# Second products of the last but one group by Strassen's form, added onto rows that stay on the chip

## The chip, the cores and the metric

One Trainium2 chip; the kernel uses one of its cores. The metric is the device time of one execution in microseconds (us). The time before is the median of 3 runs: 692.39 us (691.91 to 694.4). The engines of the core are named as the profile names them: PE (TensorE, matrix products into the accumulator banks, PSUM), DVE (VectorE), ACT (ScalarE), POOL (GpSimd, which also issues the transfers that add) and SP (SyncE, which issues the other transfers). Each of them runs its own instructions in order and waits on semaphores for the others.

## The reference

One block over x of 2048 rows and 512 columns: a modulated layer norm, a two-sided discrete Fourier transform (real part), a gated residual, a second modulated layer norm, and a gated feed-forward network with a second gated residual.

```python
mod = (_silu(c) @ w_mod).reshape(c.shape[0], 6, 1, -1)
sa, ca, ga, sb, cb, gb = (mod[:, i] for i in range(6))
h = _layernorm(x) * (1 + ca) + sa
a, b = h @ dft_hid_re.T, h @ dft_hid_im.T
x = x + ga * (dft_seq_re @ a - dft_seq_im @ b)
h = _layernorm(x) * (1 + cb) + sb
x = x + gb * ((_silu(h @ w1) * (h @ w3)) @ w2)
```

w1 and w3 are 512 x 1792, w2 is 1792 x 512, all float32. The change lies in the last product, with w2.

## The kernel before

**Tiling.** Everything is kept with the hidden columns on the partitions. The 2048 rows are four blocks t = 0 to 3 of 512 rows; the 512 output columns are four blocks d of 128; the 1792 inner columns are seven groups g = 0 to 6 of 256 (NG = 7), each as two halves q of 128. Blocks are worked in pairs, `PAIRS = ((0, 2), (1, 3))` (L814): pair 1 is the blocks 1 and 3, and it comes last. The groups 0 and 1 of pair 0 are done singly; all the rest is a list of twelve items (L1175), (2..6, pair 0) and then (0..6, pair 1).

**A product** (L96 to L106) is three matmuls, since every float32 operand is split into a high and a low part of a faster type: high x high, high x low, low x high. ScalarE copies out the high parts, VectorE subtracts to get the low ones.

**First products.** For an item, `factor` (L1362) computes the products with w1 ("a") and w3 ("b") for both blocks and both halves with seven products instead of eight, in Strassen's way; "a5" or "b3" is one of these seven, six matmuls long. Some factors add onto a PSUM bank whose earlier content ScalarE or VectorE has to have read. `result` (L1240) hands SiLU(a) times b on to the second product: the plain form makes a high and a low part of each of four tiles; `seven_parts` (L1263) makes seven pairs of parts, of the four tiles, of differences of them, through VectorE.

**Second products.** `down_unit` (L1125) is the plain form: one unit is one (t, d), six matmuls, eight units per item. `seven_unit` (L1331) is Strassen's form: seven units of six matmuls per item, each on the banks 6 and 7; a unit that opens an accumulation starts them afresh (n = 2, 5, 1), the others (3, 6, 7, 4) add onto what the unit before left there. After each unit ScalarE copies both banks, times gb, to a tile y (`copy_by`, line L335 of the profile), and GpSimd issues a transfer that adds y to the rows in DRAM, `sums[t, which]`. The units come in the order n = 2, 5, 3, 1, 6, 7, 4 and go to the places (which, k) of `TO7`: the places (0, 0), (0, 1) and (1, 1) are hit twice, (1, 0) once, by the last. Strassen's form needs sums of w2's blocks beside w2, so its weights are prepared by five background jobs (`seven_jobs`, L1294), the plain form's by two (`plain_jobs`, L1217).

**The last two groups of pair 1.** `SEVEN` (L1226) holds the groups 0 to 4 of pair 1. After the last Strassen unit of group 4 `load_sums` (L1113) reads the rows back from DRAM into four resident tiles `xr` (transfers on SP). The groups 5 and 6 use the plain form, and VectorE adds each unit, times gb, to `xr` (`own`, L1147); for group 6 SP then stores the row tile to the output. The banks of these units rotate through 6, 7, 0, 1, 2 by a count of units, `turn[1]`, that runs on from the start of the feed-forward part.

**What sets the order.** The order of units is written out by hand as strings (L1799 to L1817): "a6 y a5" is a factor, a second-product unit taken from the queue `seconds`, a factor; "-b3" is the factor b3 of the item before. Within one engine instructions run in the order in which the program emits them. `behind(n, fn)` (L1073) delays a function by n units, so that, for example, the high part of a finished tile is copied at the head of the next unit, ahead of that unit's own copies out of the banks. The background jobs go out by `advance` (L117): each unit earns credit for VectorE and ScalarE (1.36 less a fixed use per kind of unit, L1683 to L1693), and jobs are issued from the head of the queue while the credit they need is above zero. `judge` (L1013) computes the flag that decides whether a slower general branch runs; it is emitted when nine units are left in `seconds`.

Buffers in SBUF are 50 slots (`take`, `give`), used again in turn; a slot that a transfer still reads holds up who writes it next.

Of the kernel before, what the change touches and what calls it, by code (L numbers as in the profile page):

```python
# [12 lines left out]
OP = mybir.AluOpType  # L13
# [8 lines left out]
NT = S // N  # L22
ND = D // P
NG = F // (2 * P)
# [18 lines left out]
def folded(nc, pools, c, cp, wmr, wmc, x, xt, ctr, cti, wdr, wdi, w1, w3, w2, out):  # L43
# [752 lines left out]
    xr = {}  # L796
# [17 lines left out]
    PAIRS = ((0, 2), (1, 3))  # L814
    h2h, h2l = {}, {}
    xc, sums = {}, {}
# [308 lines left out]
    def down_unit(g, pair, t, d, key):  # L1125
        last = g == NG - 1

        own = pair == 1 and g >= NG - 2
        if not own and d % 2 == 0:
            ys[0] = take(F32, "y")  # L1130

        parts = 2 if own and last and (t, d) == (NT - 1, ND - 1) else 1
        for n in range(parts):
            at = slice(n * N // parts, (n + 1) * N // parts)
            to = bank(down_banks[turn[1] % len(down_banks)])[:, at]
            turn[1] += 1
            for q in range(2):
                product(
                    to,
                    [u[:, q, cols(d)] for u in wuse[key]],  # L1140
                    [hf[g, t, q][:, b, at] for b in range(2)],
                    q == 0,
                    q == 1,
                )
            if own:
                xs = xr[t][d // 2][:, d % 2, at]
                nc.vector.scalar_tensor_tensor(  # L1147
                    xs, to, gb[:, d : d + 1], xs, op0=OP.mult, op1=OP.add
                )
                if last:  # L1150
                    nc.sync.dma_start(out[t, d, :, at], xs)
            else:
                if pair == 0 and 1 <= g * ND + d <= 4:
                    nc.vector.tensor_scalar(
                        ys[0][:, d % 2, :], to, gb[:, d : d + 1], None, op0=OP.mult
                    )
                else:
                    copy_by(ys[0][:, d % 2, :], to, gb[:, d : d + 1])
        if not own and d % 2 == 1:
            y = ys.pop(0)  # L1160
            nc.gpsimd.dma_start(sums[t, d // 2], y, accum_op=OP.add)  # L1161
            behind(4, lambda: give(y))
            if last:
                behind(8, lambda i=d // 2: store(t, i))
        if d == ND - 1:
            for q in range(2):
                give(hf.pop((g, t, q)))
            if t == PAIRS[pair][1]:
                give_w(key)
            if pair == 1 and g == NG - 3:  # L1170
                load_sums(t)
# [51 lines left out]
    TO = {1: 0, 6: 0, 7: 0, 4: 0, 2: 1, 5: 2, 3: 2}  # L1223
    state, vs = {}, {}

    SEVEN = [(g, 1) for g in range(NG - 2)]  # L1226
    ORDER7 = (2, 5, 3, 1, 6, 7, 4)
    LEFT7 = {1: "h0", 2: "h2", 4: "h3", 5: "s0", 6: "s1", 7: "s2", 3: "s3"}
    TO7 = {2: (0, 0), 5: (1, 1), 3: (0, 1), 1: (0, 0), 6: (0, 1), 7: (1, 1), 4: (1, 0)}
# [101 lines left out]
    def seven_unit(g, pair, n, key):  # L1331
        new = n in (1, 2, 5)
        if new:
            banks7[:] = [bank(6), bank(7)]
        y = take(F32, "y")
        which, k = TO7[n]
        t = PAIRS[pair][k]
        names = ("h", "l") if LEFT7[n][0] == "h" else ("sh", "sl")
        u = right7.pop(((g, pair), n))
        for e, to in enumerate(banks7):  # L1340
            at = int(LEFT7[n][1]) * HALF + e * P
            product(
                to,
                [flat(wuse[key][x])[:, at : at + P] for x in names],
                [u[:, b, :] for b in range(2)],
                new,
                True,
                not new,
            )
            d = 2 * which + e  # L1350
            copy_by(y[:, e, :], to, gb[:, d : d + 1])
        give(u)
        nc.gpsimd.dma_start(sums[t, which], y, accum_op=OP.add)  # L1353
        behind(4, lambda: give(y))
        if n == ORDER7[-1]:
            for x in wuse.pop(key).values():
                give(x)
            if g == NG - 3:
                for t in PAIRS[pair]:
                    load_sums(t)  # L1360
# [322 lines left out]
    USED = {"w1": (0.0, 0.5), "w3": (1.2, 0.5), "y": (0.0, 0.6), "own": (0.7, 0.0)}  # L1683
# [7 lines left out]
    def beside(us, used):  # L1691
        advance(us - used[0], us - used[1], jobs)
        if not jobs:  # L1693
            advance(0.0, 0.0)
# [9 lines left out]
    def down(g, pair, *which):  # L1704
        key = which[-1]
        drain(lambda: (key, "l") in done, jobs)
        delayed()
        if (g, pair) in SEVEN:
            seven_unit(g, pair, *which)
        else:  # L1710
            down_unit(g, pair, *which)
        beside(1.36, USED["own" if pair == 1 and g >= NG - 2 else "y"])

    for w in ("w1", "w3"):
        load_w((w, 1))
# [36 lines left out]
    def unit(kind, i, n):  # L1752
        g, pair = items[i]
        more = i + 1 < len(items)
        if n == 1:
            drain(lambda: ("ready", i, "w1" if kind == "a" else "w3") in done, jobs)
        if (kind, i, n) == ("a", 0, 6):
            drain(lambda: ("t", 0, 4) in done)
        if (kind, i, n) == ("a", turning, 1):
            drain(lambda: not background)  # L1760
        if kind == "a" and i == turning and n in (4, 5, 6, 7):
            drain(lambda: ("t", 1, {6: 2, 5: 1, 7: 3, 4: 4}[n]) in done, jobs)
        delayed()
        factor(i, "w1" if kind == "a" else "w3", n)
        if (kind, n) == ("a", 1):
            load_w(("w1", *items[i + 1]) if more else ("w2", g, pair))
        if (kind, n) == ("a", 6):
            load_w(("w2", g, pair))
        if not more and kind == "a" and state[i, "w1"]["n"] == 7:
            down_banks[:] = [6, 7, 0, 1, 2]  # L1770
        if (kind, n) == ("a", 7 if i == turning else 3) and more:
            load_w(("w3", *items[i + 1]))
            weight_jobs(i + 1, "w1")
        if (kind, n) == ("b", 2):
            (seven_jobs if (g, pair) in SEVEN else plain_jobs)(("w2", g, pair))
        if (kind, n) == ("b", 3):
            if i + 2 == turning:
                drain(lambda: ("xc", 3) in done)
                for at in ((1, 0), (1, 1), (3, 1)):
                    chunk_parts(background, *at, 3)  # L1780
                sums_of.append(pair_sums(background, 1))
            if i + 1 == turning:
                other_operands()
            if more and not early_w3(i):
                weight_jobs(i + 1, "w3")
            if (g, pair) in SEVEN:
                seconds.extend((g, pair, n, ("w2", g, pair)) for n in ORDER7)
            else:
                for t in PAIRS[pair]:
                    seconds.extend((g, pair, t, d, ("w2", g, pair)) for d in range(ND))  # L1790
        if (kind, n) == ("b", 6) and more and early_w3(i):
            weight_jobs(i + 1, "w3")
        beside(1.36, FACTOR[kind][n])
# [4 lines left out]
    for i in range(len(items)):  # L1798
        body = "a6 a5 y y a7 y a3 y a4 y b1 y b2 y b6 b5 y"  # L1799
        if i and items[i - 1] in SEVEN:  # L1800
            body = "a6 a5 a7 y a3 a4 y b1 b2 y b6 b5 y"
        if i == turning + 1:
            body = "a6 a5 y a7 a3 y a4 b1 y b2 b6 y b5"
        spread = i > 1 and items[i - 2] in SEVEN
        if spread and i < len(items) - 1:
            body = body.replace("a6", "a6 y", 1)
        if i == len(items) - 2:
            body = "a6 y a5 y a7 a3 y a4 b1 y b2 b6 y b5"
        if i == turning:
            body = "y y y y y a6 y a5 y a7 y b1 b2 a4 b6 a3 b5"  # L1810
        if i == len(items) - 1:
            body = "a6 a5 b1 a7 a3 b2 a4 y b6 y b5 y b7 y b4 y y b3 y y y y y y y y y y"
        head = "-b7 a1 -b4 -b3 a2 " if i == turning else "-b7 a1 a2 -b4 -b3 " if i else "a1 a2 "
        if spread and i < len(items) - 1:
            head = "-b7 a1 y a2 -b4 y -b3 "
        if i == len(items) - 1:
            head = "-b7 y a1 a2 y -b4 y -b3 "  # L1817
        for at in (head + body).split():
            if at == "y":
                if (i, len(seconds)) == (len(items) - 1, 9):  # L1820
                    judge()
                if (i, len(seconds)) == (len(items) - 1, 4):
                    tc.mark_branch_hint_location("general", hint="LikelyTaken")
                down(*seconds.popleft())
            elif at[0] == "-":
                unit(at[1], i - 1, int(at[2]))
            else:
                unit(at[0], i, int(at[1]))
# [804 lines left out]
```

## Time and profile before

| what | value |
|---|---|
| median of 3 runs | 692.39 us (691.91 to 694.4) |
| the profiled execution | 690.63 us |
| its span, first to last instruction | 688.8 us |
| PE busy | 672.4 us, 98% |
| DVE busy | 586.8 us, 85% |
| ACT busy | 451.2 us, 65% |
| POOL busy | 132.2 us, 19% |
| adds of y to the rows in DRAM | 63 of 512 KB, 5.7 us from issue to landing in the median |
| read-back of the rows | 4 of 512 KB, 4.3 us from issue to landing in the median |

The shares are of the span. Matmuls are pipelined, so the length of one PE row is more than the time that it takes of PE; what a unit takes is read from start to start. In a row of the order in time a bracket at the end is the engine's idle time before the instruction and what ended it. Lines such as L87, L90, L93, L96, L100 and L335 are helpers (a copy, a difference, a sum, an elementwise product, a matmul, a scaled copy); which work it is shows in the names of the tiles.

### The profile page before, as it was taken

What the parts mean: (1) busy time and instruction counts of PE and PEld (TensorE: products, weight loads), DVE (VectorE), ACT (ScalarE), POOL (GpSimd) and SP (SyncE); (2) the same over time, 40 slices, a digit from 0 to 9 for tenths busy, and PEclk for the clock granted to TensorE, in tenths of its full rate; (3) what the DMA queues carried; (4) which work ended last, traced back from release to release, by engine and by line L of the source; (5) the groups of instructions that cost most, each with busy time, mean ns of one, the idle gap of its engine ahead of it and who ended that gap; (6) DMA issues with size and microseconds to landing.
All of it is one profiled execution on the core that took longest, in us unless ns stands there. A gap on an engine that the chain in (4) does not pass through costs nothing.

```text
span 688.8 us, 9035 instructions
## 1 busy us (share of the span) xinstructions
PE 672.4 (98%) x3122; PEld 557.4 (81%) x3122; DVE 586.8 (85%) x945; ACT 451.2 (65%) x751; POOL 132.2 (19%) x156
## 2 busy tenths in 40 slices
PE   6999999999999999999999999999999999999996
PEld 4898788888888888888788888887887888888785
DVE  5999769998999987989997989787998979888465
ACT  4998956455343665663577767867687887877620
POOL 1320162543435000100101001011011112221100
PEclk9999999999999999999999999999999999999998
DMA  8740299787679440274767666475859998999713
GB/s 264 224 124 1 54 368 339 249 297 258 197 287 291 154 151 30 46 139 122 119 141 141 150 153 121 94 128 118 267 108 183 175 203 167 181 214 173 179 45 127
DMA packets 40837, 116.80 MB, mean 170 GB/s; under 512 B 5200, under 2 KB 5456, under 8 KB 40784
## 3 DMA queue, kind: packets, MB, share of 16 engines
q0 software_dynamic: 14512, 50.86, 36.9%
q1 hardware_dynamic: 25840, 63.98, 28.1%
q10 hardware_dynamic: 432, 1.31, 0.6%
q8 instruction: 26, 0.43, 0.3%
q14 instruction: 27, 0.22, 0.1%
HBM read 76.81 MB, written 41.42 MB: 172 GB/s over the span
## 4 chain that ended last, share of the span: by engine, by line
PE 84%; DVE 9%; ACT 4%; issue 1%; DMA 1%; SPq 0%; DVEq 0%; ACTq 0%
PE bank L100 54%; PE bank L750 26%; PE bank L559 2%; PE bank L598 1%; ACT hm L501 1%; DMA x<-in_x 1%; DVE xr L806 1%; DVE st L449 1%; PE bank L576 1%; DVE v L96 1%; DVE hl L90 0%; DVE ul L90 0%; DVE x L93 0%; ACT hh L87 0%; DVE w3s L90 0%
## 5 line engine op out<-in xcount | busy, mean ns | idle before, releaser
L100 PE MATMUL bank<-hf,w2h 128*128 128x512 f32 (+1 forms) x352 | 108.3, 389 | 0.0
L87 ACT ACTIVATE hf<-v 128x512 fp32r<-128x512 f32 x71 | 44.4, 631 | 66.7 <-DVE v L96 53.9
L335 ACT ACTIVATE y<-bank,gb 128x512 f32<-128x512 f32 x118 | 76.5, 682 | 3.9 <-PE bank L100 3.6
L100 PEld LDWEIGHTS bank<-hf,w2h 128*128 128x128 f32 x352 | 65.6, 188 | 15.4 <-ACT y L335 1.5
L1161 POOL DMA_DIRECT2D sum<-y x28 | 24.0, 857 | 240.7 <-ACT y L335 124.5
L100 PE MATMUL bank<-hf,w2l 128*128 128x512 f32 (+1 forms) x176 | 68.1, 387 | 0.0
L90 DVE TENSOR_TENSOR hf<-v,hf 128x512 fp32r<-128x512 f32 x71 | 48.7, 685 | 10.6 <-ACT hf L87 10.5
L1353 POOL DMA_DIRECT2D sum<-y x35 | 29.8, 852 | 128.3 <-ACT y L335 120.8
L87 ACT ACTIVATE x<-bank 128x512 f32<-128x512 f32 x72 | 41.7, 591 | 13.6 <-PE bank L100 12.7
L750 PE MATMUL bank<-d,uh 128*128 128x512 f32 x128 | 49.9, 390 | 0.0
L750 PE MATMUL bank<-l,us 128*128 128x512 f32 x128 | 49.9, 390 | 0.0
L750 PE MATMUL bank<-d,us 128*128 128x512 f32 x128 | 49.9, 390 | 0.0
L750 PE MATMUL bank<-bh,us 128*128 128x512 f32 x128 | 49.9, 390 | 0.0
L750 PE MATMUL bank<-bh,ul 128*128 128x512 f32 x128 | 49.8, 389 | 0.0
L750 PE MATMUL bank<-l,uh 128*128 128x512 f32 x128 | 49.8, 389 | 0.0
L170 POOL DMA_INDIRECT re<-in_ctr,mirror x32 | 35.7, 1115 | 66.6 <-ACT im L188 40.1
L170 POOL DMA_INDIRECT im<-in_cti,mirror x32 | 32.9, 1028 | 33.4 <-DVE l L90 8.9
L100 PEld LDWEIGHTS bank<-hf,w2l 128*128 128x128 f32 x176 | 33.1, 188 | 6.6
L93 DVE TENSOR_TENSOR v<-bank,x 128x512 f32<-128x512 f32 x36 | 24.7, 686 | 15.6 <-PE bank L100 14.0
L1245 ACT ACTIVATE v<-v 128x512 f32<-128x512 f32 x36 | 22.6, 629 | 22.7 <-DVE v L93 22.4
L93 DVE TENSOR_TENSOR x<-bank,x 128x512 f32<-128x512 f32 x36 | 24.7, 685 | 14.5 <-PE bank L100 13.7
L188 ACT ACTIVATE im<-l 128x512 f32<-128x512 f32 x16 | 10.1, 632 | 32.4 <-DVE d L93 15.5
(260 smaller groups left out, 1922.4 us busy)
## 6 DMA issues: line engine op xcount, KB each, us to landing
sum<-y POOLq DMA_DIRECT2D x63, 512.0 KB, 5.7
w<-in_w SPq DMA_DIRECT2D x42, 512.0 KB, 4.8
re<-in_ctr SPq DMA_DIRECT2D x32, 256.0 KB, 5.8
im<-in_cti SPq DMA_DIRECT2D x32, 256.0 KB, 5.3
wmc<-in_wmc SPq DMA_DIRECT2D x8, 512.0 KB, 7.2
sum<-xr SPq DMA_DIRECT2D x8, 512.0 KB, 5.6
x<-in_x SPq DMA_DIRECT2D x11, 256.0 KB, 4.5
xr<-in_xt SPq DMA_DIRECT2D x8, 256.0 KB, 7.1
```

Source lines behind the costliest of these rows:

```text
L87: nc.scalar.activation(dst, src, AF.Copy, scale=scale)
L90: nc.vector.tensor_tensor(out=dst, in0=a, in1=b, op=OP.subtract)
L93: nc.vector.tensor_tensor(out=dst, in0=a, in1=b, op=OP.add)
L100: nc.tensor.matmul(acc, lhs[a], rhs[b], start=first and n == 0, stop=last and n == len(PASSES) - 1, skip_group_check=more,)
L170: nc.gpsimd.indirect_dma_start(dst, None, rows, bass.IndirectOffsetOnAxis(ap=at, axis=0))
L188: nc.scalar.activation(to, src.bitcast(F32), AF.Square, accum_out=chk[:, kind, KINDS.index(m), n : n + 1],)
L335: nc.scalar.activation(dst, src, AF.Identity, scale=by)
L559: nc.tensor.matmul(halves(hb[k])[:, m, :], sides((hh, hl)[a][k])[:, dt, m, :], wu[dt][:, b, m, :], start=False, stop=dt % 2 == 1 and n == ...
L750: nc.tensor.matmul(acc[what, e], lhs, rhs, start=begin and i == 0, stop=(end or (turn and what == "x")) and i == len(terms) - 1, skip_grou ...
L1161: nc.gpsimd.dma_start(sums[t, d // 2], y, accum_op=OP.add)
L1245: behind(k != 0 or q == 0, lambda: nc.scalar.activation(v, src, AF.Silu))
L1353: nc.gpsimd.dma_start(sums[t, which], y, accum_op=OP.add)
```

## The change

Group 5 of pair 1 joins `SEVEN`: its second products are seven Strassen units instead of eight plain ones. The rows are resident by then, so its seven adding transfers go to `xr` in SBUF instead of `sums` in DRAM. Only group 6 still adds on VectorE. Group 6's units are taken in another order, (t0, 0), (t0, 1), the four of t1, then (t0, 2), (t0, 3), and the unit that is split in two for the end is now (t0, 3). In the last item's string one y moves ahead of a4, and one y, ahead of b3, goes away, since there are seven units now.

```diff
     def down_unit(g, pair, t, d, key):
         last = g == NG - 1
-        own = pair == 1 and g >= NG - 2
+        own = pair == 1 and g == NG - 1
...
-        parts = 2 if own and last and (t, d) == (NT - 1, ND - 1) else 1
+        final = (t, d) == ((PAIRS[1][0] if own else PAIRS[pair][1]), ND - 1)
+        parts = 2 if own and final else 1
...
-            if t == PAIRS[pair][1]:
+            if final:
                 give_w(key)
...
-    SEVEN = [(g, 1) for g in range(NG - 2)]
+    SEVEN = [(g, 1) for g in range(NG - 1)]
...
-        nc.gpsimd.dma_start(sums[t, which], y, accum_op=OP.add)
+        to = xr[t][which] if g == NG - 2 else sums[t, which]
+        nc.gpsimd.dma_start(to, y, accum_op=OP.add)
...
-        beside(1.36, USED["own" if pair == 1 and g >= NG - 2 else "y"])
+        beside(1.36, USED["own" if pair == 1 and g == NG - 1 else "y"])
...
-                for t in PAIRS[pair]:
-                    seconds.extend((g, pair, t, d, ("w2", g, pair)) for d in range(ND))
+                t0, t1 = PAIRS[pair]
+                places = [(t, d) for t in (t0, t1) for d in range(ND)]
+                if not more:
+                    places = places[:2] + places[4:] + places[2:4]
+                seconds.extend((g, pair, t, d, ("w2", g, pair)) for t, d in places)
...
         if i == len(items) - 1:
-            body = "a6 a5 b1 a7 a3 b2 a4 y b6 y b5 y b7 y b4 y y b3 y y y y y y y y y y"
+            body = "a6 a5 b1 a7 a3 b2 y a4 y b6 y b5 y b7 y b4 y b3 y y y y y y y y y"
```

## The prediction

> **What bounds the kernel now.** I read the page first, then the order in time of TensorE (PE), VectorE (DVE) and ScalarE (ACT) from 628 us to the end, where the changed work lies.
>
> ```profile
> span 688.8 us, 9035 instructions
> PE 672.4 (98%) x3122; PEld 557.4 (81%) x3122; DVE 586.8 (85%) x945; ACT 451.2 (65%) x751; POOL 132.2 (19%) x156
> ```
>
> PE sets the time. A saving counts only as PE time, and a wait of PE counts in full. The columns below are start, length, engine, line, operation. "b3" is the third factor of w3, "y" a unit of a second product, "row unit" a `down_unit` that ends in the resident rows.
>
> ```profile
> 653.30 0.61 PE L100 MATMUL bank<-hf,w2h 128*128 128x512 f32 x2
> 666.90 0.39 PE L100 MATMUL bank<-h2h,w3sh 128*128 128x512 f32 x1
> 680.50 0.40 PE L100 MATMUL bank<-hf,w2h 128*128 128x256 f32 x2
> ...
> 636.28 0.39 PE L100 MATMUL bank<-h2h,w1h 128*128 128x512 f32 x1
> 637.42 0.39 PE L100 MATMUL bank<-h2h,w1l 128*128 128x512 f32 x1
> 637.90 0.74 PE L100 MATMUL bank<-hf,w2sh 128*128 128x512 f32 x2
> 639.40 0.39 PE L100 MATMUL bank<-th,w3h 128*128 128x512 f32 x1
> 640.93 0.73 PE L100 MATMUL bank<-hf,w2h 128*128 128x512 f32 x2
> 642.42 0.39 PE L100 MATMUL bank<-h2h,w3sh 128*128 128x512 f32 x1
> ```
>
> From the first y of group 5 (653.30) to b3 of the last item (666.90) there are ten units, from there to the last unit (680.50) ten more: 13.60 us each, so a unit of six matmuls takes 1.36 us although one row reads 0.39 (they overlap), and in this stretch PE never waits. A little earlier it does. After factor a2 (636.28) the next unit was due at 637.64 and came at 637.90; after b4 (639.40) it was due at 640.76 and came at 640.93. Each restart costs 0.13 more (637.90 to 639.40 is 1.50). Both units are Strassen units of group 4, and both add onto PSUM banks that ACT had still to copy out.
>
> **The change: the saving.** Eight units of six matmuls become seven: 1.36 us of PE. The moved y and the turned order of the row units are worth nothing on PE by themselves.
>
> **Added work on the engines, hidden.** VectorE loses eight row updates of group 5, and gets four sums of w2, one more weight split, four differences and three splits of the right operand. ScalarE gets one weight split, three operand copies and 14 copies out of PSUM, GpSimd seven issues.
>
> ```profile
> 640.00:650.00 10.00, 9.99 (x45) 7.94 (x44) 3.61 (x6) 5.45 (x10) 1.90 (x3) 1.00 1.02 207
> 643.76 0.85 POOL L1353 DMA_DIRECT2D sum<-y  x1 [1.16 <-ACT y L335]
> 644.30 0.51 POOL L1015 MEMSET sq<- 128x96 f32 x1
> 638.89 13.29 SPq L1116 DMA_DIRECT2D xr<-sum  x4
> DMA to landing us min/median/max: 3.5/6.2/7.1
> ```
>
> The window's columns after its length are PE, PEld, DVE, ACT, POOL, clock, DMA share, GB/s. The differences and splits (7 x 0.69 us) come where DVE is busy 3.61 of 10 us; without that room they would be 4.8 us. The rows are read back by 652.18 plus one landing; the add that needs the last of them comes after the second y, at about 659. On GpSimd, in order, an add can wait for an earlier add to the same place (two y units and two factors, 5.4 us, lie between such a pair, against a median landing of 6.2) and behind the adds stands the judge's clearing (0.51): it is done about 1.1 us after b3, and VectorE asks for it at 1.57. SP's stores follow the turned row units one for one.
>
> **Added work on the path, first place: the weights of w2.** Helpers issue background jobs while their credit lasts. A unit adds 1.36 less its own use, and with no job waiting the credit is capped at 1.0. Before, both jobs of this w2 go out after b2. Now five do, and I carried the credits through the seven units that follow. After b2: w2's high copy and sums (DVE credit 0.56 to -0.84). After b6: w2's lows and high copy of the sums. After y: the sums' lows and w3's high copy. After b5: w3's sums. After b7: nothing (-1.0). After the next y: w3's lows and the high copy of its sums. After a1: their lows. Before, all of w3 stood ahead of b7's two VectorE instructions; now its last two VectorE jobs stand behind them, among the instructions that PE's next two units wait for.
>
> ```profile
> 628.39 0.69 DVE L93 TENSOR_TENSOR x<-bank,x 128x512 f32<-128x512 f32 x1 [1.24 <-PE bank L100]
> 629.73 1.22 DVE L90 TENSOR_TENSOR w2l<-w,w2h 128x1024 fp32r<-128x1024 f32 x1
> 630.87 0.42 DVE L93 TENSOR_TENSOR w3s<-w 128x256 f32<-128x256 f32 x1
> 632.33 0.68 DVE L90 TENSOR_TENSOR hf<-v,hf 128x512 fp32r<-128x512 f32 x1
> 632.93 1.21 DVE L90 TENSOR_TENSOR w3l<-w,w3h 128x1024 fp32r<-128x1024 f32 x1
> 634.07 1.22 DVE L90 TENSOR_TENSOR w3sl<-w3s,w3sh 128x1024 fp32r<-128x1024 f32 x1
> 635.20 0.68 DVE L93 TENSOR_TENSOR x<-bank,x 128x512 f32<-128x512 f32 x1
> 635.92 0.69 DVE L96 TENSOR_TENSOR v<-v,x 128x512 f32<-128x512 f32 x1
> 638.95 0.69 DVE L93 TENSOR_TENSOR v<-bank,x 128x512 f32<-128x512 f32 x1 [0.95 <-ACT x L87]
> ...
> 632.95 1.06 ACT L87 ACTIVATE w3sh<-w3s 128x1024 fp32r<-128x1024 f32 x1
> 636.64 0.63 ACT L87 ACTIVATE hf<-v 128x512 fp32r<-128x512 f32 x1 [2.15 <-DVE v L96]
> 637.18 1.25 ACT L335 ACTIVATE y<-bank,gb 128x512 f32<-128x512 f32 x2
> 638.32 0.59 ACT L87 ACTIVATE x<-bank 128x512 f32<-128x512 f32 x1
> 639.67 0.63 ACT L1245 ACTIVATE v<-v 128x512 f32<-128x512 f32 x1 [0.76 <-DVE v L93]
> 640.21 1.25 ACT L335 ACTIVATE y<-bank,gb 128x512 f32<-128x512 f32 x2
> ```
>
> Start to start, a split of 128x1024 takes 1.14, four sums 1.46 (630.87 to 632.33), hf 0.60. From 629.73 DVE now has sums, split, hf, split, sums: 1.46 + 1.14 + 0.60 + 1.13 + 1.46 = 5.79, so b7's x starts at 635.52 instead of 635.20. ACT's hf, its two y copies and PE's next unit shift by the same 0.32: PE restarts at 638.22. ACT's pair is over for the next instruction at 638.64. There stands w3's copy of the sums now (until 639.70); x follows at 639.60, not 638.32. DVE, in order, holds the split of the sums for that copy (639.72), and a2's sum starts at 640.86 instead of 638.95: 1.91 late. SiLU (639.67) and the two y copies behind it (640.21) are as late, and PE's unit of 640.93 starts at 642.84. **Plus 1.91 us.** A bound below is 0.32 (the late copy finds ACT free), one above 1.91 + 1.14 (one more split ahead).
>
> **Second place: copies between units that share banks.** In the last item a Strassen unit's two copies stand on ACT behind an hf copy that needs the factor before it.
>
> ```profile
> 668.46 0.69 DVE L93 TENSOR_TENSOR x<-bank,x 128x512 f32<-128x512 f32 x1 [0.61 <-PE bank L100]
> 669.19 0.69 DVE L96 TENSOR_TENSOR v<-v,x 128x512 f32<-128x512 f32 x1
> 670.49 0.41 DVE L1016 TENSOR_REDUCE sq<-chk 128x8 f32<-128x256 f32 x1
> 673.50 0.67 DVE L90 TENSOR_TENSOR hf<-v,hf 128x512 fp32r<-128x512 f32 x1
> ...
> 669.91 0.63 ACT L87 ACTIVATE hf<-v 128x512 fp32r<-128x512 f32 x1 [4.11 <-DVE v L96]
> ```
>
> b3 ends on PE at 666.90 + 1.36 = 668.26; hf starts 1.65 later. With hf to y of 0.54 (636.64 to 637.18), the first copy would run from 2.19 to 2.87 after the factor's end, the second to 3.44. Where two units follow the factor, the third is due at 2.72 and waits for the first copy: 0.19 + 0.13 = 0.32. That is b2, y, a4, y and b7, y, b4, y: **plus 0.64 us**; below 0 if DVE is a little early, above 1.3 if each is half a unit late.
>
> After b3 the last Strassen unit is followed at once by the first row unit. The turn of the banks has stood at 56 since the first half of the work; 56 mod 5 picks bank 7, the bank of that Strassen unit's second half. The row unit is due at 1.36 and gets its bank at 3.44 + 0.04: 2.12 + 0.13, **plus 2.25 us**. The lower bound is 0 (a free bank), the upper 3.5 with one more 1.25 us pair ahead.
>
> The judge's small instructions (670.49 to 673.50, 3.01 us) now stand ahead of the low half that the third row unit needs. They would end 1.57 + 3.01 + 0.69 = 5.27 after b3; that unit's second matmul, due at 4.31 unstalled, comes at 6.56 behind the stall. So they cost nothing, but 1.0 us if that cover goes.
>
> **The adds on the chip** are not in the trace of before. The nearest rows are the adds into `sum`, 3.5 to 7.1 us from issue to landing; I take the median 6.2. The last is issued about 3.7 after b3's end and its rows are updated after 13.3, so 9.6 us are allowed: zero, and 4.6 if it took twice the longest.
>
> [...]
>
> ```profile
> 680.00:689.00 9.00, 2.10 (x15) 1.77 (x14) 1.78 (x4) 0.00 (x0) 0.00 (x0) 0.79 0.31 108
> ```
>
> The clock reads 1.00 through the short waits above, and under 1 only in this window, in which PE ends at 682.1.
>
> **The sum.** -1.36 + 1.91 + 0.64 + 2.25 = +3.44 us. The span goes from 688.8 to 692.2, the profiled execution from 690.63 to 694.1; the median of the runs, 692.39, lies 1.76 above that execution, and I put the same sum on it: 695.8 us, 0.5% more.
>
> **Rivals.**
> *Part of it* (694.0): one of the two large waits is absent. Without the bank wait the judge's 1.0 shows: +2.2 (694.6). Without the late weights: +1.5 (693.9). For it: each hangs on one order of instructions. Against: both orders follow from the code and the rows.
> *The saving arrives, not slower* (691.0): ACT reaches the y copies early enough everywhere, so that PE takes 1.36 less. This needs hf copies that do not stand ahead of y copies; it decides at a copy end of 1.32 after the factor (now 3.44). The two old waits (0.26 and 0.17 with restarts 0.69) could go too: 690.3. Against it is the pair of waits that already stands at 637.90 and 640.93.
> *Slower by more* (699): the adds onto the rows land later than 9.6 us after issue. Both ends of the transfer lie in SBUF, and each of three places takes two adds. At twice the longest landing, 14.2, the last rows come 4.6 late: 3.44 + 4.6 gives 700.4; a bank wait longer by a pair of copies gives 697.
> *It doesn't do what it says* (692.4): the last group's rows and the fewer units cancel, no wait changes.
>
> **How the numbers follow.** Forecast 0.50, part 0.22, saving 0.12, slower by more 0.12, nothing 0.04. The range 691.4 to 698.2 holds nearly all of the first, second and last, part of the slow case, and leaves out half of the saving. A change of 0.5% (3.46 us: below 688.93 or above 695.85) is about what a measurement of this kernel can tell. My forecast sits at that bound. Half of its 0.50 and all of "slower by more" come out above: slower 0.38. Faster by 0.5% needs more than every saving named, 2.05 us: 0.04 for what I don't see. The rest, 0.58, is no change.
>
> **What would show it.** In the changed trace: about 2 us between b4 and group 4's last unit, released by ACT's y; w3's copy of the sums on ACT behind a y pair; about 2 us ahead of the first row unit, released by ACT's y; short gaps at the second and sixth Strassen unit of group 5; no VectorE row update that waits for an add. If PE runs without gaps through the last 60 us, or if the adds hold VectorE, I am wrong.

## The result

The changed kernel takes 695.7 us (median of 9 runs, 694.33 to 697.28) against 691.91 us (9 runs of the kernel before, 690.8 to 694.4): ratio 1.005, 95% interval 1.0035 to 1.0064, that is 2.4 to 4.4 us more. The forecast was 695.8 us, 3.44 more.

The profiled execution of the changed kernel is slower than its median, and it has to be taken apart before it is read: 697.28 us, 6.7 us of span more than before.

Page of the changed kernel:

```profile
span 695.5 us, 9061 instructions
PE 674.9 (97%) x3116; PEld 557.3 (80%) x3116; DVE 588.7 (85%) x949; ACT 463.0 (67%) x769; POOL 138.6 (20%) x163
```

PE issues six matmuls fewer, and the span is 6.7 us longer all the same. VectorE is 1.9 us busier, ScalarE 11.8. One part of the 6.7 us has nothing to do with the change. The first fence is ScalarE's order in time before the change, the second after it, both in the Fourier stage:

```profile
100.55 0.63 ACT L342 ACTIVATE scr<-scr 128x512 f32<-128x512 f32 x1 [3.07 <-DMA scr<-in_c]
```

```profile
102.14 0.63 ACT L342 ACTIVATE scr<-scr 128x512 f32<-128x512 f32 x1 [3.93 <-DMA scr<-in_c]
```

The same instruction waits for the same transfer and comes 1.6 us later, and from there to b2 of group 5's item the instructions of ScalarE and VectorE are about 1.5 us late (1.47 to 1.60 for most of them). Such shifts differ from execution to execution (the eleven others of this study lie between 0.2 us early and 2.8 us late at b2). So the stages are compared by a stretch that starts where the change starts: from the start of VectorE's sum after that b2 to the start of the last matmul. Before, that is 628.39 (shown in the prediction) to this row:

```profile
681.82 0.28 PE L100 MATMUL bank<-hf,w2l 128*128 128x256 f32 x1
```

53.43 us. The changed kernel, VectorE, ScalarE and PE in order of time:

```profile
629.91 0.69 DVE L93 TENSOR_TENSOR x<-bank,x 128x512 f32<-128x512 f32 x1 [1.24 <-PE bank L100]
631.25 0.42 DVE L93 TENSOR_TENSOR w2s<-w 128x256 f32<-128x256 f32 x1
637.05 0.68 DVE L93 TENSOR_TENSOR x<-bank,x 128x512 f32<-128x512 f32 x1
639.52 0.69 DVE L90 TENSOR_TENSOR hf<-v,hf 128x512 fp32r<-128x512 f32 x1
641.26 1.23 DVE L90 TENSOR_TENSOR w3sl<-w3s,w3sh 128x1024 fp32r<-128x1024 f32 x1 [1.06 <-ACT w3sh L87]
642.40 0.69 DVE L93 TENSOR_TENSOR v<-bank,x 128x512 f32<-128x512 f32 x1
...
639.04 1.25 ACT L335 ACTIVATE y<-bank,gb 128x512 f32<-128x512 f32 x2
640.18 1.05 ACT L87 ACTIVATE w3sh<-w3s 128x1024 fp32r<-128x1024 f32 x1
643.12 0.63 ACT L1246 ACTIVATE v<-v 128x512 f32<-128x512 f32 x1 [1.40 <-DVE v L93]
643.66 1.25 ACT L335 ACTIVATE y<-bank,gb 128x512 f32<-128x512 f32 x2
674.20 0.63 ACT L87 ACTIVATE hf<-v 128x512 fp32r<-128x512 f32 x1 [2.01 <-DVE v L96]
674.74 1.25 ACT L335 ACTIVATE y<-bank,gb 128x512 f32<-128x512 f32 x2
...
639.76 0.73 PE L100 MATMUL bank<-hf,w2sh 128*128 128x512 f32 x2 [0.43 <-ACT y L335]
644.38 0.74 PE L100 MATMUL bank<-hf,w2h 128*128 128x512 f32 x2 [1.59 <-ACT y L335]
658.40 0.73 PE L100 MATMUL bank<-hf,w2sh 128*128 128x512 f32 x2
669.68 0.73 PE L100 MATMUL bank<-hf,w2sh 128*128 128x512 f32 x2
676.04 0.73 PE L100 MATMUL bank<-hf,w2h 128*128 128x512 f32 x2 [1.97 <-ACT y L335]
688.60 0.28 PE L100 MATMUL bank<-hf,w2l 128*128 128x256 f32 x1
```

The stretch is 688.60 - 629.91 = 58.69 us, 5.26 more. The bracket of 644.38 is the wait ahead of group 4's last Strassen unit, that of 676.04 the wait ahead of the first row unit; both name ScalarE's copy of y. How much later than due a unit starts is read from PE's pitch of 0.227 us per matmul: 0.59 and 1.75 us at group 4's last two units (639.76 and 644.38; before: 0.25 and 0.17), 0.24 at 658.40, 0.26 at 669.68, 2.13 at 676.04, and 0.11 to 0.14 for each restart. (A bracket is shorter than that by about 0.16 us: it counts from the modelled end of the matmul before, whose row reads 0.39 us against the pitch of 0.227.) That makes 5.59 us, against 0.67 before; less the 1.36 us of the unit that is gone it is 3.56 us more. 1.70 us of the 5.26 are left. They lie where PE's clock was halved:

```profile
677.40:680.60 3.20, 3.20 (x9) 2.55 (x8) 1.15 (x3) 0.00 (x0) 0.00 (x0) 0.50 0.99 189
```

This window (columns as in the prediction) lies behind the wait of 676.04. PE is busy throughout, but shows 9 matmuls in 3.2 us (16 in such a window at full clock, further down), at a granted clock of 0.50.

### The profile page after: what moved, and what is told of

Read it like the earlier page. It is cut to its first block, busy times and chain, and to the rows that moved or that the text cites. A ratio compares the mean times of both kernels' runs of the same rounds, so it can differ in the third digit from the quotient of the medians.

```text
span 695.5 us, 9061 instructions
## 1 busy us (share of the span) xinstructions
PE 674.9 (97%) x3116; PEld 557.3 (80%) x3116; DVE 588.7 (85%) x949; ACT 463.0 (67%) x769; POOL 138.6 (20%) x163
## 4 chain that ended last, share of the span: by engine, by line
PE 75%; DVE 12%; DMA 4%; ACT 4%; issue 2%; SPq 1%; ACTq 0%; DVEq 0%
PE bank L100 52%; PE bank L750 19%; PE bank L559 2%; DMA scr<-in_c 1%; DMA wmr<-in_wmr 1%; PE bank L598 1%; DVE v L96 1%; DVE x L93 1%; ACT y L335 1%; DMA w<-in_wdi 1%; SPq L231 1%; DVE xr L806 1%; DVE d L93 1%; DVE ul L90 1%; DVE l L90 1%
## 5 line engine op out<-in xcount | busy, mean ns | idle before, releaser
L100 PE MATMUL bank<-hf,w2h 128*128 128x512 f32 (+1 forms) x332 | 103.4, 393 | 3.6 <-ACT y L335 3.6
L335 ACT ACTIVATE y<-bank,gb 128x512 f32<-128x512 f32 x132 | 85.7, 682 | 4.1 <-PE bank L100 3.6
L87 ACT ACTIVATE hf<-v 128x512 fp32r<-128x512 f32 x74 | 46.1, 630 | 59.6 <-DVE v L96 48.2
L100 PEld LDWEIGHTS bank<-hf,w2h 128*128 128x128 f32 x332 | 62.6, 190 | 18.8 <-ACT y L335 5.4
L100 PE MATMUL bank<-hf,w2l 128*128 128x512 f32 (+1 forms) x166 | 65.0, 391 | 0.0
L90 DVE TENSOR_TENSOR hf<-v,hf 128x512 fp32r<-128x512 f32 x74 | 50.6, 685 | 11.4 <-ACT hf L87 11.3
L100 PEld LDWEIGHTS bank<-hf,w2l 128*128 128x128 f32 x166 | 31.5, 190 | 6.4
```

Of the source, the lines that this page charges most:

```text
L87: nc.scalar.activation(dst, src, AF.Copy, scale=scale)
L90: nc.vector.tensor_tensor(out=dst, in0=a, in1=b, op=OP.subtract)
L100: nc.tensor.matmul(acc, lhs[a], rhs[b], start=first and n == 0, stop=last and n == len(PASSES) - 1, skip_group_check=more,)
L335: nc.scalar.activation(dst, src, AF.Identity, scale=by)
```

## The experiments

My theory: the added w2 jobs push w3's behind what PE waits for; the first row unit waits for the bank of the unit before it; the adds on the chip cost nothing. The rivals: the adds cost the time, or the added engine work as such does, wherever it stands.

| kernel | median us | ratio to before (95%) | stretch, us | against before | clock 0.50 behind the wait |
|---|---|---|---|---|---|
| before | 691.91 | | 53.43 | | no |
| changed | 695.7 | 1.005 (1.0035 to 1.0064) | 58.69 | +5.26 | yes |
| first row unit on bank 0 | 693.86 | 1.0031 (1.0018 to 1.0044) | 55.89 | +2.46 | no |
| w2 jobs after b4 | 694.66 | 1.004 (1.0023 to 1.0056) | 55.46 | +2.03 | no |
| adds left out | 697.07 | 1.0069 (1.005 to 1.0088) | 58.63 | +5.20 | yes |
| bank, jobs, judge | 692.58 | 1.0004 (0.9993 to 1.0016) | 53.21 | -0.22 | no |
| copies ahead of hf | 694.02 | 1.0021 (1.0008 to 1.0033) | 55.94 | +2.51 | no |
| two more copies | 698.72 | 1.0094 (1.0072 to 1.0116) | 59.47 | +6.04 | yes |
| one more copy | 698.64 (one run) | | 59.13 | +5.70 | yes |
| changed, second execution | 697.12 (one run) | | 57.06 | +3.63 | no |
| changed, third execution | 694.19 (one run) | | 57.06 | +3.63 | no |
| all waits removed | 690.46 | 0.9981 (0.9968 to 0.9993) | 51.75 | -1.68 | no |
| before, jobs reordered | 691.96 | 1.0002 (0.9986 to 1.0017) | 52.72 | -0.71 | no |

The stretches are of one profiled execution each, the ratios of 6 to 12 runs against 9 to 29 of the kernel before on the same chip.

### The bank of the first row unit

```diff
-            down_banks[:] = [6, 7, 0, 1, 2]
+            down_banks[:] = [0, 1, 2, 6, 7]
+            turn[1] = 0
```

> Edit: the row units of the last item start at bank 0 instead of bank 7; nothing else. Theory (banks and job order): the 2.1 us wait ahead of the first row unit goes, with its restart 2.25 us, and with it the stretch at half clock that followed it in the profiled execution of the change (1.7 us); the judge's instructions then hold the third row unit for about 1.0 us. The wait ahead of group 4's last Strassen unit (about 1.6 us) stays. Time against the changed kernel (695.7 us) lower by 1.2 to 2.9: 692.8 to 694.5. Rival (the adds onto the rows hold the end, or the adds slow the end): no row unit waits less, 695.7.

693.86 us. The wait ahead of the first row unit is gone, and in its place PE waits at the third:

```profile
676.62 0.50 PE L100 MATMUL bank<-hf,w2h 128*128 128x512 f32 x1 [0.81 <-DVE hf L90]
```

This matmul is 0.97 us late and is released by the low half on VectorE, which stands behind the judge. The stretch falls by 58.69 - 55.89 = 2.80 us; from the terms it should be 2.13 + 0.12 + 1.70 (clock) - 0.97 - 0.10 = 2.88. Against the executions of the changed kernel at full clock (57.06 us, further down) it falls by 1.17 us, where the terms give 1.18. Bank and judge are as the prediction had them; 1.8 us in the medians lie inside the range expected.

### The place of the w2 jobs

```diff
-        if (kind, n) == ("b", 2):
+        if (kind, n) == ("b", 4 if i == len(items) - 2 else 2):
             (seven_jobs if (g, pair) in SEVEN else plain_jobs)(("w2", g, pair))
```

> Edit: the five weight jobs for group 5's w2 are queued after factor b4 of group 5 instead of after b2; nothing else. Theory: w3's jobs of the last item go out earlier than before the change, so both waits of group 4's last two Strassen units go: 1.9 us against the changed kernel for the one, 0.7 for what stood there already before the change. The wait ahead of the first row unit stays with about 2.1 us. 695.7 less 2.6: 693.1. Rival (the adds are the cause): 695.7. Rival (more work on ScalarE and VectorE as such, wherever it stands): the wait turns up elsewhere, 695.7.

694.66 us, 1 us less instead of 2.6, and by its interval not to be told from the changed kernel; what the edit did shows in the stretch. It is 55.46 us, 1.60 less than the changed kernel takes at full clock (57.06). The added wait went: ahead of group 4's last two units the delays are 0.31 and 0.15 us, as before the change. At the unit after y, a4 (the second of the short waits, 658.40 above) the delay rose from 0.24 to 0.48 us. The two old waits stayed, which the expectation had wrong. The kernel with bank, jobs and judge changed together has the same order there, and its VectorE shows why:

```profile
634.15 1.23 DVE L90 TENSOR_TENSOR w3sl<-w3s,w3sh 128x1024 fp32r<-128x1024 f32 x1 [0.88 <-ACT w3sh L87]
635.29 0.68 DVE L93 TENSOR_TENSOR x<-bank,x 128x512 f32<-128x512 f32 x1
```

With w2's jobs out of the way, w3's last split now waits for ScalarE's copy, which stands behind a pair of y copies, and b7's sum starts at 635.29, where it started at 635.20 before. The time was not set by how much VectorE had to do, but by the order on ScalarE. The wait ahead of the first row unit is there with the same length, and no half clock follows it in this execution:

```profile
675.33 0.74 PE L100 MATMUL bank<-hf,w2h 128*128 128x512 f32 x2 [1.97 <-ACT y L335]
```

### Without the adds

```diff
-        nc.gpsimd.dma_start(to, y, accum_op=OP.add)
+        if g != NG - 2:
+            nc.gpsimd.dma_start(to, y, accum_op=OP.add)
```

> Edit: the seven transfers that add group 5's results onto the resident rows are not issued, so group 5 of pair 1 is missing from two blocks' results; all products and copies stay. Theory: the adds land before their rows are updated, so nothing waits for them, and the time is that of the changed kernel, 695.7 us. Rival (the adds cost): lower by more than 2 us.

697.07 us, not less than the changed kernel, and the stretch agrees with it to 0.06 us. The transfers of the changed kernel, in its list of transfers:

```profile
sum<-y POOLq DMA_DIRECT2D x63, 512.0 KB, 5.3
xr<-y POOLq DMA_DIRECT2D x7, 512.0 KB, 5.4
```

An add onto rows in SBUF lands 5.4 us after issue in the median, an add into DRAM 5.3. In the changed kernel's list of waits nothing but one later add waits for them:

```profile
DVE xr L1148 <- PE bank L100: 5.5, 8, 1.8
POOL xr L1355 <- DMA xr<-y: 1.9, 1, 1.9
```

The row updates wait for PE alone. The rival that the adds cost the time falls. That the median lies above the changed kernel's by 1.4 us is not explained by the stretch and stays open.

### Bank, jobs and judge together

The two edits above, and the judge's instructions at the point where six units are left. That point comes twice in this program (once among group 5's units, once among the row units), so they run twice, beside PE both times.

```diff
-                if (i, len(seconds)) == (len(items) - 1, 9):
+                if (i, len(seconds)) == (len(items) - 1, 6):
                     judge()
```

> Edit: both of the above (bank 0 for the first row unit, the w2 jobs after b4), and the judge's instructions three units later. Theory: all large waits go, only the two of 0.3 us behind the hf copies stay; from the sum +3.44 less 1.91, 0.69 and 2.25: 1.4 us less than the kernel before, 690.5 us, and no half clock. Rival (adds, or more engine work as such): no better than the kernel before, 692 to 694.

692.58 us, 2 us more than expected and no difference from the kernel before. Three of the expected terms came: the wait for the bank, the late weights and the judge's 1.0 us are gone from the stretch. The old waits (0.30 and 0.14 with their restarts 0.71) stayed, and the unit after y, a4 was 0.45 late instead of 0.24. From the terms: -1.36 + 0.58 + 0.38 + 0.04 = -0.36, measured -0.22. The unit saved was eaten by what was left.

### The copies ahead of the hf copy

```diff
+        if (g, pair, which[0]) == (NG - 2, 1, 4):
+            seven_unit(g, pair, *which)
+            delayed()
+            return beside(1.36, USED["y"])
         delayed()
```

> Edit: for the last Strassen unit of group 5 the delayed functions are issued after the unit instead of ahead of it, so that its two copies out of the banks stand ahead of the hf copy of b3 on ScalarE; the first row unit keeps bank 7. Theory: the second copy then ends about 2.2 us after b3 instead of 3.44, and the wait ahead of the first row unit falls from 2.12 to about 0.9 us: 1.2 us less than the changed kernel, and no half clock after it: 692.8 to 694.5. Rival (the bank is not what the row unit waits for, but the hf part or the adds): wait unchanged, 695.7.

694.02 us. PE's start of the first row unit:

```profile
675.49 0.74 PE L100 MATMUL bank<-hf,w2h 128*128 128x512 f32 x2 [0.78 <-ACT y L335]
```

0.93 us late where 0.9 was worked out, and no half clock behind it. So the wait is made of two things that can be taken away one by one: the bank, and the place of ScalarE's copies behind the hf copy.

### A longer wait, and the clock

```diff
+        if (g, n) == (NG - 2, 4):
+            for e in range(2):
+                copy(y[:, e, :], u[:, 0, :].bitcast(F32))
         for e, to in enumerate(banks7):
```

A second kernel has one such copy instead of two.

> Edit: two more ScalarE copies of 128x512 from SBUF, written to the y tile and overwritten, stand ahead of the copies of group 5's last Strassen unit. Theory: the wait ahead of the first row unit grows by their 1.1 us from 2.1 to 3.2 us. If the stretch at half clock comes from the length of that wait, it is there again and as long or longer: 696.8 to 698.5. Rival (the half clock is chance and has nothing to do with the wait): wait longer by 1.1, no half clock, 695.1 to 696.8 with its chance as before.

> One more ScalarE copy (instead of two) ahead of the copies of group 5's last Strassen unit. Theory: wait ahead of the first row unit 2.13 + 0.55 = 2.7 us. If the half clock depends on the length of the wait and on chance, it is likelier here than after 2.1 us; if a wait of fixed length sets it, it is there as surely as after 2.1.

PE in the kernel with two copies, then its window behind the wait:

```profile
675.66 1.22 PE L100 MATMUL bank<-hf,w2h 128*128 128x512 f32 x2 [3.00 <-ACT y L335]
675.80:679.00 3.20, 3.20 (x8) 2.53 (x9) 0.93 (x2) 0.00 (x0) 0.85 (x1) 0.54 0.68 131
```

And with one copy:

```profile
677.37 1.22 PE L100 MATMUL bank<-hf,w2h 128*128 128x512 f32 x2 [2.63 <-ACT y L335]
677.50:680.70 3.20, 3.20 (x9) 2.54 (x9) 1.25 (x4) 0.00 (x0) 0.85 (x1) 0.55 0.84 157
```

The units start 3.16 and 2.78 us late, as worked out (3.2 and 2.7), and both have a stretch at half clock, here from the first matmul on. The time with two copies, 698.72 us, lies just above the 698.5 that was given as its upper end. The changed kernel itself was profiled in two more executions:

> The changed kernel once more, for its clock alone. Theory: the wait of 2.1 us ahead of the first row unit is there to a few hundredths, since it follows from the order of instructions; the half clock behind it comes in some executions and not in others, and costs 1.7 us where it comes. Rival: it comes always, as in the first profile.

> The same again: a third look at the wait and at the clock behind it, with the same expectation of each theory.

697.12 and 694.19 us. Windows behind the wait, in this order:

```profile
678.40:681.60 3.20, 3.20 (x16) 2.64 (x15) 2.07 (x4) 0.00 (x0) 0.00 (x0) 1.00 1.01 188
```

```profile
675.70:678.90 3.20, 3.20 (x16) 2.64 (x15) 2.13 (x4) 0.00 (x0) 0.03 (x1) 1.00 1.02 189
```

Each starts its row unit 2.13 us late, as in the first profile, at full clock; both stretches are 57.06 us, 3.63 more than before, 1.63 less than the stretch with the half clock. So the wait is fixed and the clock is not: behind 2.13 us it fell in 2 of 5 profiled executions (0.50 in the first of the changed kernel and 0.52 without the adds, there from 675.50 to 678.70; 1.00 in the changed kernel's two others and with the jobs moved), behind 2.78 and 3.16 in both, behind 1.78 or less in none. What decided it behind 2.13 us is not shown.

### All waits removed, and the kernel before with the same order of jobs

On the changed kernel: bank 0, the judge among group 5's units, w2's jobs after b4, and

```diff
-        if (kind, n) == ("b", 6) and more and early_w3(i):
+        if (kind, n) == ("b", 2 if i == len(items) - 2 else 6) and more and early_w3(i):
             weight_jobs(i + 1, "w3")
...
+        if (g, pair) == (NG - 2, 1):
+            seven_unit(g, pair, *which)
+            delayed()
+            return beside(1.36, USED["y"])
         delayed()
```

> Edit: first row unit on bank 0, judge emitted at group 5's second Strassen unit, group 5's w2 jobs after b4, the last item's w3 jobs after b2 instead of b6, and in group 5's Strassen units the delayed functions after the unit. Theory: all waits from b2 of group 5's item on go, also the 0.7 us that the kernel before has; 1.36 and 0.69 less than before: 689.8 us against 691.85, with an unbroken row of matmuls. Rival (extra engine work or the adds slow what surrounds them): 691 to 693.

> Edit, on the kernel before: only the order of the weight jobs as in the run that combines all (w3 after b2, w2 after b4); group 5 stays plain. Theory: the two old waits go, 0.7 us less than before: 691.2; the difference to the combined run is the pure worth of seven units for eight, 1.36 us. Rival (the old waits come from something else than the weight jobs): 691.85.

690.46 us, ratio 0.9981 (0.9968 to 0.9993): this version beats both kernels, the one before by little (1.3 us by the ratio, 0.5 to 2.2). The stretch is 51.75 us, and one wait is left in it:

```profile
655.71 0.73 PE L100 MATMUL bank<-hf,w2sh 128*128 128x512 f32 x2
```

The kernel before with the jobs reordered has no wait left; its stretch is 0.71 shorter, its median the same as before (0.9986 to 1.0017: a gain of 0.7 us can't be told from none). Between the two stretches lie 0.97 us: 1.36 for the unit, less 0.25 and 0.11 for the wait shown, which makes 1.00. So the worth of seven units for eight is what six matmuls take on PE, and no more.

With this the second rival falls too. This version gives the engines the work of the changed kernel (VectorE 588.0 us in 949 instructions against 588.7, ScalarE 462.7 in 769 against 463.0), and only the order differs. The added work as such costs nothing in this stretch.

## Why the prediction was right

**The saving.** -1.36 us: right; it is seen alone in the last two kernels (0.97 with a wait of 0.36 against it).

**First place, the weights of w2.** +1.91 was predicted from the order of jobs; 2.60 us of delay and restart now stand where 0.67 stood, +1.93. The chain is the predicted one, row by row: b7's sum 0.3 later after the shift of 1.5, w3's copy of the sums behind the y pair (640.18), its split held up (641.26, 1.06 us), a2's sum after it, SiLU and y copies after that, PE at 644.38. Moving the jobs took it away.

**Second place.** +0.64 for the two short waits; 0.36 and 0.38 were measured. +2.25 for the bank of the first row unit; 2.13 and 0.12 were measured. The judge's 1.0 us, covered as long as that wait stands, showed with 0.97 as soon as it went.

**The adds.** Zero, as predicted: 5.4 us to landing against the 9.6 allowed and the 6.2 taken. The row behind that 6.2 (3.5/6.2/7.1) mixes the adds with the read-back of the rows; the adds alone took 5.2 to 7.1 us there, which changes nothing in the term.

**The sum.** +3.44 predicted; the two later profiles of the changed kernel give +3.63, the medians +3.8, the ratio +3.5 (2.4 to 4.4 by the interval). That the absolute times agree to 0.1 us (695.8 and 695.7) is partly luck: the forecast stood on 692.39 us, the median of three runs, which nine runs put 0.48 us lower, and the change came out 0.35 larger in the medians than the sum. The two errors nearly cancel. The chances put the result at the mark of 0.5%, and there it lies.

**What was not right** is the clock: the sum carried no term for it. The runs show a granted clock of 0.50 after the wait of 2.13 us in 2 of 5 executions, worth 1.6 to 1.7 us. Over many executions that would be some 0.7 us (2/5 of 1.7, an estimate from these five). The medians can't show it, since the interval of the change is 2 us wide; that the spread between executions comes from it is not shown either, since the early shifts are as large.

**Among the rivals**, *part of it* (693.9 to 694.6) is the range that the kernels with one cause removed measured, but crosswise: without the bank wait 694.6 was put and 693.86 measured, without the late weights 693.9 and 694.66. The intervals of the two overlap; by the stretches (+2.46 and +2.03 us against before) the order is the one predicted (+2.2 and +1.5). *The saving arrives* was put at 691.0, or 690.3 with the old waits gone; the version that removes all measured 690.46. *Slower by more* through late adds has no support left.

## What to carry to other kernels

A saving of matmuls on the bounding engine is worth its pitch (six times 0.227 us here), and has to be held against every wait that the new form adds: units that add onto the banks of the unit before them need the copy engine's order, instruction by instruction, to be worked out with them. Where work is queued by credit, follow the new queue through the next units before asking whether an engine has room; in the window that the prediction quotes, VectorE was busy for 3.61 and ScalarE for 5.45 of 10 us, and PE was held by their order all the same. After a move, look which bank, buffer or helper instruction (here the judge) now stands one place nearer to the bounding engine.

## What the runs showed of the hardware that I had not expected

PE's clock fell to 0.50 behind waits of PE of 2.13 us (2 of 5 executions), 2.78 and 3.16 us (each once), and not behind those of 1.78 us or less. It cost 1.6 to 1.7 us behind 2.13 us and 1.4 behind the longer waits (the stretch less 57.06 and the added wait). In the changed kernel it set in 1.2 us after the restart of 676.04, at 677.25, and stayed for 3.41 us, to 680.66; with the longer waits it was there from the first matmul on (the first two take 1.22 us, where they take 0.73 at a clock of 1.00).

The kernel with one more copy showed the same at the start of the program, where PE waits for x from VectorE (L485): the idle time there was 2.58 us, and the clock read 0.50 behind it. In the kernel before it was 1.81 us and in the changed kernel's first profile 0.85, and the clock stayed at 1.00 (8.00 to 18.00 us in both). The row and the window with one more copy:

```profile
10.66 0.60 PE L485 MATMUL bank<-ident,x 128*128 128x128 f32 x3 [2.58 <-DVE x L470]
11.40:14.60 3.20, 3.20 (x9) 1.67 (x9) 3.06 (x5) 2.60 (x5) 0.00 (x0) 0.50 1.00 241
```

Transfers of 512 KB that add onto rows in SBUF took as long as those that add into DRAM (5.4 and 5.3 us from issue to landing in the median, seven and 63 of them in the changed kernel).
